# Two attention-and-MLP layers on one core: a new order for the first four tiles, a residual kept in PSUM at the end, and a DMA queue scheduled with new estimates of issue times

## The chip, the cores and the metric

The kernel runs on one core of one Trainium2 chip. The metric is the time of one execution on the device in microseconds (us), lower is better. A profile is of one execution, and its span is a few us shorter than that execution's time. Engine names are those of the profile: PE (TensorE matmul), PEld (its weight load), DVE (VectorE), ACT (ScalarE), POOL (GpSimd), SPq (the queue of DMA issues of the sync engine). "PEclk" is the TensorE clock that was granted, 1.00 being full speed.

## The reference

```python
def reference(A_x, A_wqkv, A_wo, B_x, B_w1, B_b1, B_w2, B_b2):   # x: 1 x 2048 x 512, bf16
    # _A_ref: qkv = x @ wqkv, 32 heads of 16; softmax(q k^T / 4) v; @ wo
    # _B_ref: gelu(layernorm(x) @ w1 + b1) @ w2 + b2, hidden 1376   (it normalises its input once more)
    x = A_x
    x = x + _A_ref(_layernorm(x), A_wqkv, A_wo)                          # "L = 1" in the kernel
    x = x + _B_ref(_layernorm(x), B_w1, B_b1, B_w2, B_b2)
    x = x + _A_ref(_layernorm(x), A_wqkv, A_wo)                          # "L = 3"
    x = x + _B_ref(_layernorm(x), B_w1, B_b1, B_w2, B_b2)
    return x
```

Two times 32 x 2048 x 2048 exponentials make up most of the work.

## The kernel before

The kernel is a generator of instructions. Jobs (Python generators) submit tasks with a priority (the lower number goes first) and with **estimated durations**. A list scheduler plays these estimates forward and, for each engine, takes the ready task of the lowest priority number; if none is ready it takes the one that is ready first. What comes out is a fixed order of some 43,000 instructions, in which each engine waits in program order. The estimates do no work on the chip, but they decide the order.

```python
    def op(self, eng, fn, reads=(), writes=(), same_ok=(), dur=0.3, lat=None):
        ...
        if eng == "sp":                                     # a DMA: dur = time on the queue,
            self.free[eng] = op.t0 + dur
            op.t1 = op.t0 + dur + (2.0 if lat is None else lat)   # lat = from there to the landing
    ...
    def best(self, e):                                      # choice of the next task of engine e
        lim = self.P.free[e] + self.LOOK[e]
        for t in self.pend[e]:
            r = self.task_ready(t)
            if r <= lim: k = (t.prio, t.seq)                # ready: lowest (prio, seq)
            else:        k = (r, t.prio, t.seq)             # none ready: the earliest
    ...
    def dma(self, fn, reads, writes, prio, dur=0.08, lat=None):
        return Task("sp", prio, [I(fn, reads, writes, dur, (), lat)])
```

All DMAs go through one queue. The ones that matter here:

```python
        ld = lambda fn, writes: self.dma(fn, [], writes, 2.0, 0.1, 4.0)            # MLP weights
        ...
        yield self.dma(lambda e: e.dma_start_transpose(xnT, xnr), [RX], [RXT], prio, 0.9)   # tokens
        ...
            # query transposes, one for each segment of (512 queries, 4 heads):
            yield self.dma(... dma_start_transpose(self.qraw..., self.q_scr...), ..., 1.5, 0.9 * sg["W"] / 512)
        ...
    def job_kload(self, hg):        # second attention: keys and values of 12 token tiles come back from DRAM
        yield ("keys", [(k, 3, tt) for k in ("ks", "vs") for tt in range(12)])
        yield self.dma(lambda e: e.dma_start_transpose(self.KT[:, hg:hg + 1, 0:1536], self.k_scr[...]), ..., 1.4, 2.6)
        yield self.dma(lambda e: e.dma_start(self.V[:, hg, 0:12, ...], self.v_scr[...]), ..., 1.4)   # dur 0.08
```

At the start, each of the first four token tiles did keys, queries and values in one job and took the norms of queries and keys in one reduction; the rows of the softmax bound (`qt`, five small operations) went to POOL. In the first attention the other 12 tiles follow behind, while 64 exponentials of the first four tiles' pairs run.

Of the kernel before, what the change touches and what calls it, by code (L numbers as in the profile page):

```python
# [8 lines left out]
BF16 = mybir.dt.bfloat16  # L9
# [442 lines left out]
class Builder:  # L452
# [44 lines left out]
    def alloc(self, es):  # L497
# [44 lines left out]
        self.n2 = t("n2", [128, 2, 64], F32)  # L542
        self.n2k = t("n2k", [128, NT, 32], BF16)
        self.nm = t("nm", [128, 32], BF16)
        self.qy = t("qy", [128, 2, 32], I32)
        self.qt1 = t("qt1", [128, 2, 32], F32)
        self.qt2 = t("qt2", [128, 2, 32], F32)
# [27 lines left out]
        pl["sq"] = Pool(range(3))  # L575
        pl["n2"] = Pool(range(2))
# [17 lines left out]
    def sqs(self, s):  # L594

        if s == 0:
            return self.sq0[:, :].rearrange("p (h c) -> p h c", c=16)
        return (self.h16[:, 8:10, :] if s == 1 else self.OT[:, 6:8, :]).rearrange("p a (h c) -> p (a h) c", c=16)
# [73 lines left out]
    def build_startup_late(self):  # L672
# [4 lines left out]
        def fills():  # L677
# [18 lines left out]
            ld = lambda fn, reads, writes: self.dma(fn, reads, writes, 4.0, 0.4, 5.0)  # L696
# [30 lines left out]
    def flow_weights(self):  # L727
# [3 lines left out]
        ld = lambda fn, writes: self.dma(fn, [], writes, 2.0, 0.1, 4.0)  # L731

        def first(fc):
            M = 128 if fc < nf else self.FLAST
            dst = self.wf[:, fc, 0:4 * M].rearrange("p (c m) -> p c m", m=M)
            return ld(lambda e: e.dma_start(dst, wr1[:, :, fc * 128:fc * 128 + M]), [("wf", fc)])

        def second(L, fc):
            W = self.w2res(L, fc) + ([("wqkv", fc % 3)] if L == 3 else [])
            M = 128 if fc < nf else self.FLAST  # L740
            yield ld(lambda e: e.dma_start(self.w2(L, fc)[0:M, :], self.B_w2[fc * 128:fc * 128 + M, :]), W)
            if fc == nf:
                yield ld(lambda e: e.dma_start(self.w2(L, fc)[M:M + 1, :], self.B_b2.rearrange("(o n) -> o n", o=1)), W)
# [47 lines left out]
    def job_lnqkv(self, L, tiles, prio, later=None):  # L791
# [4 lines left out]
        for i, tt in enumerate(tiles):  # L796
            self.S_.spawn(self.job_qkv_tile(L, tt, slot, i, left, prio + 0.01 * i, "qkv" if later is None else "kv"), prio + 0.01 * i)
# [5 lines left out]
    def job_qkv_tile(self, L, tt, slot, i, left, prio, what):  # L803
        S_ = self.S_
        direct = (L == 1) or tt >= 12
        start = (L == 1 and tt < 4)
        if start:
            xnr, RX = self.dp[:, 4 + tt // 2, (tt % 2) * 512:(tt % 2) * 512 + 512].bitcast(BF16), ("xs", tt)
            xnT, RXT = self.yT[:, :, tt * 128:(tt + 1) * 128], ("yT", tt)
        else:  # L810
            xr = yield ("get", "xn")
            xnr, RX = self.xn[:, xr, :], ("xn", xr)
# [4 lines left out]
        if not start:  # L817
            xs = yield ("get", "xnT")
            xnT, RXT = self.xnT[:, xs, :, :], ("xnT", xs)
        yield self.dma(lambda e: e.dma_start_transpose(xnT, xnr), [RX], [RXT], prio, 0.9)  # L820
        if not start:
            S_.release("xn", xr)
# [7 lines left out]
        def kstore():  # L830
            if direct:
                yield self.dma(lambda e: e.dma_start_transpose(self.KT[:, :, tt * 128:(tt + 1) * 128], self.qks(qs)[:, 1, :]), [QK], [("kt", hg, tt) for hg in range(8)], prio, 1.75)
            else:
                yield self.dma(lambda e: e.dma_start(self.k_scr[tt * 128:(tt + 1) * 128, :], self.qks(qs)[:, 1, :]), [QK], [("kscr", tt)], prio)
            S_.mark(("ks", L, tt))

        def vstore(vs):
            yield self.dma(lambda e: e.dma_start(self.v_scr[tt * 128:(tt + 1) * 128, :], self.vst[:, vs, :]), [("vst", vs)], [("vscr", tt)], prio)
            S_.release("vst", vs)
            S_.mark(("vs", L, tt))  # L840
# [6 lines left out]
        if start:  # L847
            ss = yield ("get", "sq")
        if "k" in what:
# [3 lines left out]
            if start:  # L853
                yield Task("act", prio, [I(lambda e, b=b: e.activation(out=self.sqs(ss)[:, 32:64, :], in_=kdst, func=ACTF.Square), [QK], [("sq", ss, 1)], 0.65)])
            S_.release("mb", b)
            S_.spawn(kstore(), prio)
        if "q" in what:
# [3 lines left out]
            if start:  # L861
                yield Task("act", prio, [I(lambda e: e.activation(out=qdst, in_=qsrc, func=ACTF.Copy, scale=0.25 * YU), [("ps", b)], [QQ], 0.65),
                                         I(lambda e: e.activation(out=self.sqs(ss)[:, 0:32, :], in_=qsrc, func=ACTF.Square, scale=0.25 * YU), [("ps", b)], [("sq", ss, 0)], 0.65)])
            else:
                yield Task("dve", prio, [I(lambda e: e.tensor_scalar(out=qdst, in0=qsrc, scalar1=0.25 * YU, scalar2=None, op0=ALU.mult), [("ps", b)], [QQ], 0.68)])
            S_.release("mb", b)
        if "v" in what:
# [3 lines left out]
            if direct:  # L871
# [3 lines left out]
                if start:  # L875
                    yield Task("act", prio, [I(lambda e: e.activation(out=vdst, in_=psv, func=ACTF.Copy), [("ps", b)], VR, 0.65)])
                else:
                    yield Task("dve", prio, [I(lambda e: e.tensor_copy(out=vdst, in_=psv), [("ps", b)], VR, 0.68)])
# [7 lines left out]
        if not start:  # L886
            S_.release("xnT", xs)
        if not start:
            ss = yield ("get", "sq")
# [7 lines left out]
        if not start:  # L897
            yield Task("dve", prio, [I(lambda e: e.tensor_tensor(out=sq, in0=v4, in1=v4, op=ALU.mult), [("qk", qs, k) for k in range(k0, k1)], SR, 0.12 + 0.0085 * N)])
        yield Task("dve", prio, [I(lambda e: e.tensor_reduce(out=self.n2[:, ns, h0:h1], in_=sq, axis=AX.X, op=ALU.add), SR, [("n2", ns)], 0.12 + 0.017 * N)])
        S_.release("sq", ss)  # L900
        if "k" in what:
            yield Task("dve", prio, [I(lambda e: e.tensor_copy(out=self.n2k[:, tt, :], in_=self.n2[:, ns, 32:64]), [("n2", ns)], [("n2k", tt)], 0.18)])
            S_.mark(("n2k", L, tt))
        if "q" in what:
            yield Task("dve", prio, [I(lambda e: e.tensor_scalar(out=self.qy[:, ns, :], in0=self.n2[:, ns, 0:32].bitcast(I32), scalar1=-0.5, scalar2=RSQRT_MAGIC, op0=ALU.mult, op1=ALU.add), [("n2", ns)], [("qy", ns)], 0.18)])
            y = self.qy[:, ns, :].bitcast(F32)
            a, c, x = self.qt1[:, ns, :], self.qt2[:, ns, :], self.n2[:, ns, 0:32]
            RA, RC, RX = ("qt1", ns), ("qt2", ns), ("n2", ns)
            yield Task("pool", prio, [I(lambda e: e.tensor_tensor(out=a, in0=x, in1=y, op=ALU.mult), [RX, ("qy", ns)], [RA], 0.35)])
            yield Task("pool", prio, [I(lambda e: e.tensor_tensor(out=c, in0=a, in1=y, op=ALU.mult), [RA, ("qy", ns)], [RC], 0.3)])  # L910
            yield Task("pool", prio, [I(lambda e: e.tensor_scalar(out=c, in0=c, scalar1=-0.5, scalar2=1.5, op0=ALU.mult, op1=ALU.add), [RC], [RC], 0.28)])
            yield Task("pool", prio, [I(lambda e: e.tensor_tensor(out=a, in0=a, in1=c, op=ALU.mult), [RA, RC], [RA], 0.3)])
            yield Task("pool", prio, [I(lambda e: e.tensor_scalar(out=pads(self.qks(qs)[:, 0, :])[:, :, 16:17], in0=a.rearrange("p (n o) -> p n o", o=1), scalar1=-MARG, scalar2=0.0, op0=ALU.mult, op1=ALU.add),
                                        [RA], [QQ], 0.4)])
# [3 lines left out]
        if "q" in what:  # L918
            li = L // 2
            if start:  # L920
                yield Task("pe", 0.5, [I(lambda e: e.transpose(self.psbf(self.q0bank)[:, tt * 128:(tt + 1) * 128], self.qks(qs)[:, 0, 0:128], self.ident[:, :]), [QQ, ("ident",)], [("ps", self.q0bank)], 0.1, [("ps", self.q0bank)])])
                S_.mark(("q0", tt))
            yield self.dma(lambda e: e.dma_start(self.q_scr[li, tt * 128:(tt + 1) * 128, :], self.qks(qs)[:, 0, :]), [QQ], [("qscr", L, tt)], prio)
            S_.mark(("qst", L, tt))
        S_.release("qk", qs)

# [22 lines left out]
    def flow_q(self):  # L949
        for sg in self.segs:  # L950
# [6 lines left out]
            else:  # L957
# [3 lines left out]
                               [("qscr", L, tt) for tt in sg["toks"]], [("qraw", s)], 1.5, 0.9 * sg["W"] / 512)  # L961
# [32 lines left out]
    def job_kload(self, hg):  # L994
# [3 lines left out]
                       [("kscr", tt) for tt in range(12)], [("kt", hg, kb) for kb in range(12)], 1.4, 2.6)  # L998
        yield self.dma(lambda e: e.dma_start(self.V[:, hg, 0:12, :, :].rearrange("p k h d -> p k (h d)"), self.v_scr[0:1536, hg * 68:(hg + 1) * 68].rearrange("(k p) c -> p k c", p=128)),
                       [("vscr", tt) for tt in range(12)], [("V", hg, kb) for kb in range(12)], 1.4)  # L1000
# [319 lines left out]
    def job_segend(self, sg):  # L1320
# [20 lines left out]
        if nparts == 2 and part == 0:  # L1341
# [4 lines left out]
            yield Task("pool", 1.2, [I(lambda e: e.tensor_copy(out=M, in_=T[:, :, 0:16]), [RA], [RO] + [("sq", 2, i) for i in (0, 1)], 0.5), I(lambda e: e.tensor_copy(out=den, in_=T[:, :, 16]), [RA], [RD], 0.2)])  # L1346
# [26 lines left out]

    def job_post(self, L, qc):
        S_ = self.S_
        pr = 0.95 if (L, qc) == (1, self.NC - 1) else 2.2
# [28 lines left out]
    def job_yt(self, L, tt, slot, i, left, pr):  # L1405
# [6 lines left out]
        yield self.dma(lambda e: e.dma_start_transpose(self.yT[:, :, i * 128:(i + 1) * 128], self.xn[:, xr, :]), [("xn", xr)], [("yT", i)], pr, 0.9)  # L1412
# [222 lines left out]
```

## Time and profile before

| | before |
|---|---|
| time, median (lowest to highest) | 1698.29 us (1695.0 to 1700.98), 3 runs |
| profiled span | 1695.3 us, mean granted PE clock 0.988 |
| ACT busy / idle in the span | 1580.9 / 114.4 us |
| exponentials of ACT | 1322 in number, idle directly before them 81.6 us |

ACT is the engine to watch. Its busy time in stretches shows where its idle time lies; the columns are the stretch, its length, ACT's busy time with the number of instructions, the PE clock, the DMA share and GB/s:

```profile
0.00:98.00 98.00, 69.35 (x80) 1.00 0.67 137
98.00:130.00 32.00, 20.29 (x19) 0.79 0.48 102
130.00:850.00 720.00, 702.29 (x613) 1.00 0.16 38
850.00:895.00 45.00, 34.43 (x31) 0.92 0.68 114
895.00:1660.00 765.00, 736.58 (x639) 0.99 0.09 22
```

The length less the busy time is the idle time: 28.7, 11.7, 17.7, 10.6 and 28.4 us. The two short stretches lose far more in proportion than the long ones of the bulk. These are the two rows of ACT's timeline that the start and the first short stretch turn on (start, busy time, operation, count; in brackets the idle time before the row and what ended it):

```profile
32.54 10.19 ACT L1113 ACTIVATE PT<-ps 128x1024 bf16<-128x1024 f32 x11 [7.86 <-PE ps L1128]
...
106.21 1.02 ACT L1113 ACTIVATE PT<-ps 128x1024 bf16<-128x1024 f32 x1 [8.05 <-PE ps L1128]
```

The second short stretch is the layer switch, where the queue and the wait of DVE read like this (start, time on the queue, operation, count; then waiter, releaser, total, times, longest):

```profile
843.78 14.85 SPq L997 DMA_TRANSPOSE KT<-k_scr  x7
858.73 9.00 SPq L999 DMA_DIRECT2D V<-v_scr  x7
...
872.02 5.43 SPq L960 DMA_TRANSPOSE qraw<-q_scr  x3
```

```profile
DVE QT L972 <- DMA qraw<-q_scr: 8.6, 1, 8.6
```

All reloads go first, the query transposes last, and DVE stands still for 8.6 us for a query transpose.

### The profile page before, as it was taken

Reading aid. Unit: us, or ns where it says so; the run is one execution under the profiler, and the core shown is the slowest. Engines: PE = TensorE matmul, PEld = TensorE weight load, DVE = VectorE, ACT = ScalarE, POOL = GpSimd, SP = SyncE. Lnnn points to the kernel's source line nnn. Section 1 sums busy time; section 2 is a strip of 40 time slices with the busy share of each in tenths; the row PEclk is TensorE's granted clock in tenths of the full one; section 3 lists DMA queues with packets and bytes.
Section 4 is the critical chain, followed back from the end, with each engine's and each line's share of the span. In section 5 each row is a group of like instructions: output and inputs, shape, how many; then the busy total and the mean of one; then the engine's idle time right before and its main releaser. Section 6 shows DMA issues by size and latency. Waiting matters only on the chain.

```text
span 1695.3 us, 43536 instructions
## 1 busy us (share of the span) xinstructions
PE 1618.0 (95%) x18235; PEld 543.4 (32%) x18235; DVE 1456.1 (86%) x3164; ACT 1580.9 (93%) x1400; POOL 384.0 (23%) x640
## 2 busy tenths in 40 slices
PE   8989999999999999999989999999999999999998
PEld 5222322222222332232223323323222222344444
DVE  6869999988898799988949799988899989988894
ACT  4879999999998999999979999899999999999995
POOL 4045421101211112111122124411011101223220
PEclk9989999999999999999999999999999999999999
DMA  6662000102102211102372230010000100000000
GB/s 165 112 112 64 23 8 8 39 19 56 55 22 48 41 55 33 30 28 44 79 119 55 57 82 20 18 20 8 17 8 8 20 12 8 7 19 7 22 7 14
DMA packets 181249, 66.52 MB, mean 39 GB/s; under 512 B 160859, under 2 KB 175424, under 8 KB 181056
## 3 DMA queue, kind: packets, MB, share of 16 engines
q1 hardware_dynamic: 181056, 63.75, 17.0%
q8 instruction: 146, 2.39, 0.6%
q14 instruction: 47, 0.39, 0.1%
HBM read 19.96 MB, written 15.30 MB: 21 GB/s over the span
## 4 chain that ended last, share of the span: by engine, by line
PE 60%; ACT 30%; DVE 6%; DMA 2%; issue 1%; SPq 1%; POOL 0%; DVEq 0%; POOLq 0%
ACT PT L1113 27%; PE ps L1128 22%; PE ps L1297 17%; PE ps L844 4%; PE ps L1420 4%; PE ps L1458 4%; PE ps L1038 4%; PE ps L1387 3%; DVE dp L1205 2%; DVE dp L1236 2%; ACT h L1450 2%; PE ps L1041 1%; DMA yT<-xn 1%; DVE accT L1327 1%; DMA xnT<-xn 0%
## 5 line engine op out<-in xcount | busy, mean ns | idle before, releaser
L1113 ACT ACTIVATE PT<-ps 128x1024 bf16<-128x1024 f32 (+1 forms) x1322 | 1505.8, 1256 | 81.6 <-PE ps L1128 75.8
L1128 PE MATMUL ps<-QT,KT 32*128 32x512 bf16 (+1 forms) x4608 | 678.4, 359 | 53.1 <-ACT PT L1113 21.3
L1205 DVE TENSOR_SCALAR dp<-ps 128x512 uint16<-128x512 f32 x824 | 557.8, 684 | 121.2 <-PE ps L1128 114.0
L1236 DVE TENSOR_SCALAR dp<-dp 128x1024 uint16<-128x1024 uint16 (+1 forms) x1257 | 490.4, 432 | 10.9 <-PE ps L1297 6.6
L1297 PE MATMUL ps<-PT,V 128*17 128x512 bf16 (+1 forms) x3674 | 472.0, 361 | 0.2 <-DVE accT L1327 0.2
L989 POOL TENSOR_SCALAR vs<-V 128x340 bf16<-128x340 bf16 (+3 forms) x312 | 258.3, 833 | 866.1 <-PE ps L1297 817.4
L1297 PE MATMUL ps<-dp,vs 128*17 128x512 bf16 (+1 forms) x2802 | 408.2, 357 | 0.4 <-DVE dp L1236 0.4
L1128 PEld LDWEIGHTS ps<-QT,KT 32*128 32x128 bf16 x4608 | 178.5, 91 | 578.7 <-issue 172.5
L1297 PE MATMUL ps<-dp,V 128*17 128x512 bf16 (+1 forms) x934 | 195.7, 358 | 2.4 <-DVE accT L1327 2.2
L1038 PE MATMUL ps<-wqkv,zw 128*32 128x256 bf16 x4432 | 188.2, 275 | 0.8 <-DVE accT L1327 0.8
L1297 PEld LDWEIGHTS ps<-PT,V 128*17 128x17 bf16 x3674 | 111.3, 88 | 114.9 <-issue 102.2
L1297 PEld LDWEIGHTS ps<-dp,vs 128*17 128x17 bf16 x2802 | 102.4, 89 | 111.2 <-issue 95.3
L1038 PEld LDWEIGHTS ps<-wqkv,zw 128*32 128x32 bf16 x4432 | 105.8, 96 | 80.3 <-issue 60.8
L1420 PE MATMUL ps<-yT,wf 128*128 128x512 bf16 (+3 forms) x396 | 104.8, 369 | 4.8 <-DMA yT<-xn 3.9
L844 PE MATMUL ps<-wqkv,xnT 128*128 128x512 bf16 x336 | 95.2, 391 | 8.8 <-DMA xnT<-xn 8.8
L1327 DVE STREAM_TRANSPOSE accT<-ps 128x512 f32<-128x512 f32 (+1 forms) x88 | 58.1, 661 | 23.5 <-PE ps L1297 22.2
L1444 DVE TENSOR_SCALAR h<-ps,b1c 128x512 bf16<-128x512 f32 (+2 forms) x88 | 61.7, 701 | 9.3 <-PE ps L1420 8.8
L1387 PE MATMUL ps<-wo,OT 128*128 128x512 bf16 x240 | 68.0, 387 | 0.2 <-DVE dp L1205 0.2
L1297 PEld LDWEIGHTS ps<-dp,V 128*17 128x17 bf16 x934 | 48.1, 88 | 43.4 <-issue 26.7
L1420 PEld LDWEIGHTS ps<-yT,wf 128*128 128x128 bf16 (+1 forms) x396 | 28.5, 100 | 59.2 <-issue 30.1
L972 DVE TENSOR_SCALAR QT<-qraw,scl,qbias 128x512 bf16<-128x512 bf16 (+1 forms) x87 | 37.3, 431 | 10.3 <-DMA qraw<-q_scr 10.0
L1367 DVE STREAM_TRANSPOSE OT<-ob 128x512 bf16<-128x512 bf16 (+1 forms) x72 | 45.9, 639 | 0.1
(154 smaller groups left out, 801.9 us busy)
## 6 DMA issues: line engine op xcount, KB each, us to landing
wf<-in_B_w_dram SPq DMA_DIRECT2D x90, 128.0 KB, 2.5
q_scr<-qk SPq DMA_DIRECT2D x22, 256.0 KB, 2.2
k_scr<-qk SPq DMA_DIRECT2D x12, 256.0 KB, 2.0
out_dram<-xres SPq DMA_DIRECT2D x16, 128.0 KB, 1.7
v_scr<-vst SPq DMA_DIRECT2D x12, 136.0 KB, 2.0
V<-v_scr SPq DMA_DIRECT2D x8, 204.0 KB, 4.9
wqkv<-in_A_wqkv_dram SPq DMA_DIRECT2D x3, 512.0 KB, 4.2
q_scr<-h SPq DMA_DIRECT2D x6, 256.0 KB, 3.1
```

The costliest lines, as they stand in the source:

```text
L844: yield Task("pe", prio, [I(lambda e, c=c: e.matmul(self.ps[:, b, :], lhsT=xnT[:, c, :], rhs=self.wqkv[:, c, which * 512:which * 512 + 512 ...
L989: yield Task("pool", 0.8, [I(lambda e, k=k: e.tensor_scalar(out=self.vs[:, q, k - 1, i:i + n, :], in0=src, scalar1=WSHIFT[k], scalar2=None ...
L1038: P.op("pe", lambda e, p=p: e.matmul(self.ps[p:p + 32, b, 0:w], lhsT=self.zw[:, 0:32], rhs=rhs[:, 0:w], start=st, stop=st, skip_group_chec ...
L1113: S_.submit(Task("act", 1e-5 * gi, [I(lambda e, pt=pt, n=n, b0=b0: e.activation(out=self.PT[:, pt:pt + n, :], in_=self.ps[:, b0:b0 + n, :] ...
L1128: return [I(lambda e, kb=kb, i=i: e.matmul(self.ps[:, b, i * W:(i + 1) * W], lhsT=self.KT[32 * hp:32 * hp + 32, hg, kb * 128:(kb + 1) * 12 ...
L1205: self.S_.submit(Task("dve", 0.0, [I(lambda e: e.tensor_scalar(out=self.dp[:, u, w * 512:(w + 1) * 512], in0=self.ps[:, b, :], scalar1=BIT ...
L1236: yield Task("dve", pr, [I(lambda e, k=k, v=v: e.tensor_scalar(out=self.dp[:, v, 0:N], in0=self.dp[:, u, 0:N], scalar1=float(SHIFT[k]), sc ...
L1297: ops.append((i, I(lambda e, hp=hp, v=v, ap=ap[:, i * W:(i + 1) * W], first=first and i == 0, W=W: e.matmul(self.ps[32 * hp:32 * hp + 17, ...
L1327: yield Task("dve", 0.3, [I(lambda e: e.transpose(self.accT[:, a, 0:W], self.ps[:, ACCB, 0:W]), [("ps", ACCB)], [RA], 0.15 + 0.53 * W / 512)])
L1387: yield Task("pe", pr, [I(lambda e, hg=hg, i=i, b=b: e.matmul(self.ps[:, b, :], lhsT=self.OT[:, hg, i * 128:(i + 1) * 128], rhs=self.wo[:, ...
L1420: yield Task("pe", pr, [I(lambda e, c=c: e.matmul(self.ps[0:M, b, off:off + W], lhsT=self.w1(fc, c), rhs=self.yT[:, c, 0:W], start=(c == 0 ...
L1458: yield Task("pe", pr, [I(lambda e, fc=fc, i=i, b=b: e.matmul(self.ps[:, b, :], lhsT=self.gt(fc, i, W), rhs=self.w2(L, fc), start=(fc == 0 ...
```

## The change

The intent has three parts. **Start:** in the first four tiles, keys and their norms come first, queries next, values last; the last tile's bound rows go to DVE, and there are more buffers for squares and norms. **Queue:** the DMAs get new estimates, meant to be the issue times of a trace. Also, MLP weights fall behind (priority 3.0), query transposes pass the reloads (1.3 against 1.4); the MLP of the third unit of the first layer is raised from 2.2 to 1.6. **Tail:** the last tokens' residual is put into PSUM by an identity matmul, so that two adds fall away, and 14 output projections no longer go ahead of the last attention matmuls. Cut to its core:

```diff
-        ld = lambda fn, writes: self.dma(fn, [], writes, 2.0, 0.1, 4.0)
+        ld = lambda fn, writes, dur, prio: self.dma(fn, [], writes, prio, dur, 3.5)
-            return ld(lambda e: e.dma_start(dst, wr1[...]), [("wf", fc)])
+            return ld(lambda e: e.dma_start(dst, wr1[...]), [("wf", fc)], 0.75, 3.0)
-        yield self.dma(lambda e: e.dma_start_transpose(xnT, xnr), [RX], [RXT], prio, 0.9)
+        yield self.dma(lambda e: e.dma_start_transpose(xnT, xnr), [RX], [RXT], prio, 1.25)
-            (key transposes 1.75, key, value and query stores 0.08)
+            (key transposes 2.4,  key, value and query stores 0.45)
-                               [...qscr...], [("qraw", s)], 1.5, 0.9 * sg["W"] / 512)
+                               [...qscr...], [("qraw", s)], 1.3, 0.1 + 1.1 * sg["W"] / 512)
-                       [...kscr...], [...kt...], 1.4, 2.6)
+                       [...kscr...], [...kt...], 1.4, 2.0)
-                       [...vscr...], [...V...], 1.4)
+                       [...vscr...], [...V...], 1.4, 1.3, 3.5)
+    def post_prio(self, L, qc):
+        return 0.95 if (L, qc) == (1, self.NC - 1) else 1.6 if (L, qc) == (1, self.NC - 2) else 2.2
 ... first four tiles
+    def job_first_tile(self, tt, slot, i, left, prio):
+        ...                       # three jobs for each tile
+        S_.spawn(keys(), prio)            # its tasks at prio - 0.3: 4 matmuls, copy, square, reduce of 32 norms
+        S_.spawn(queries(), prio)         # 4 matmuls, copy and square on ACT, reduce; bound rows on "dve" if tt in (3,)
+        S_.spawn(values(), prio + 1.0)    # 4 matmuls, copy on ACT
 ... tail
+        yield Task("pe", 1.5, [... matmul(ps[b], lhsT=ident, rhs=xres[tt], start=True, stop=False ...)])
-            yield Task("pe", pr, [... matmul(ps[b], OT, wo, start=(hg == 0), stop=(hg == 7)) ...])
+            yield Task("pe", pr if h0 == 7 else 1.5, [... matmul(ps[b], OT, wo, start=False, stop=(hg == 7)) ...])
-        yield Task("dve", pr, [... tensor_tensor(xres = ps + xres) ...])
-        yield Task("dve", pr, [... bn_stats(st, in_=xres) ...])
+        yield Task("dve", pr, [... bn_stats(st, in_=ps) ...])
 ... (second MLP matmuls add into the same bank; the two last adds become copies, one on DVE, one on ACT)
```

## The prediction

> **What bounds the kernel now.** I read the page first (busy shares, 40 slices), then ScalarE's (ACT) groups with shapes kept apart, then the ACT exponentials by stretches of 10 and 20 us to find where they stop, then the timelines of ACT and of the DMA queue (SPq) around each stop, and the chain for the two ends of the kernel.
>
> ```profile
> PE 1618.0 (95%) x18235; PEld 543.4 (32%) x18235; DVE 1456.1 (86%) x3164; ACT 1580.9 (93%) x1400; POOL 384.0 (23%) x640
> L1113 ACT ACTIVATE PT<-ps 128x1536 bf16<-128x1536 f32 x629 | 930.6, 1479 | 46.1 <-PE ps L1128 40.7
> L1113 ACT ACTIVATE PT<-ps 128x1024 bf16<-128x1024 f32 x692 | 723.5, 1053 | 35.5 <-PE ps L1128 35.1 <-PE ps L942 0.2
> ```
>
> The bulk is softmax exponentials on ACT. The union of all of them is 1506 us of 1695. PE's 95% contains filler matmuls (188 us at one line alone), so the real limit in the bulk is ACT, with DVE and PE close behind. ACT idles 1695.3 - 1580.9 = 114 us in all, 81.6 us of it directly before exponentials. The change cannot shorten an exponential, so what it can win lies in that idle time and in the work before the first and after the last exponential.
>
> ```profile
> 100.00:120.00 20.00, 10.39 (x10) 0.66 0.42 89
> ...
> 510.00:520.00 10.00, 6.78 (x7) 0.83 0.28 44
> ...
> 870.00:880.00 10.00, 2.82 (x3) 0.73 0.66 130
> ...
> 1070.00:1080.00 10.00, 6.72 (x7) 1.00 0.12 27
> 1130.00:1140.00 10.00, 7.17 (x8) 0.70 0.23 47
> ...
> 1520.00:1530.00 10.00, 5.63 (x5) 0.66 0.10 21
> ```
>
> These are stretches (first line exponentials alone, the others all of ACT): length, busy time and count, granted PE clock, DMA share, GB/s. Outside them ACT is mostly above 9 in 10. Almost every hole has a lowered PE clock, so PE had stopped too. The queue shows why for the first big one:
>
> ```profile
> 89.35 0.56 SPq L697 DMA_DIRECT2D bst<-in_B_b_dram  x1
> 89.96 0.23 SPq L698 DMA_DIRECT2D bst<-in_B_b_dram  x1
> 90.23 1.75 SPq L701 DMA_DIRECT2D wo<-in_A_wo_dram  x4
> 92.02 8.13 SPq L736 DMA_DIRECT2D wf<-in_B_w_dram  x11
> 100.26 3.85 SPq L820 DMA_TRANSPOSE xnT<-xn  x3
> ```
>
> For 10.9 us the single queue issues weights that nobody needs for hundreds of us, while transposes of normalised tokens stand behind them. PE, in order, waits 6.9 us for the first transpose, and ACT waits 8.05 us before its exponential at 106.2, then 2.0 us more while PE is at a low clock.
>
> **What the Trainium skill says.** "DMA: Bandwidth & Descriptors", Anatomy of one DMA: a semaphore wait of a DMA happens on the issuing sequencer, before dispatch, and the fixed cost is about 2 us, mostly completion. The trace agrees on head-of-line blocking (above), but gives the issue cost itself as the problem: 8.13/11 = 0.74 us per weight load, 6.01/4 = 1.5 us per token transpose, 9.00/7 = 1.29 us per V reload. The scheduler in the kernel assumed 0.1, 0.9 and 0.08. "TensorE: Matmul & The Clock Gate", HAM oscillation: an idle gap of over about 3.4 us halves the PE clock. The trace agrees: four matmuls that take 0.97 us in the chain took 1.89 us after the 6.9 us gap. "VectorE: DVE Perf Modes", Why PSUM operands drop a tier: a PSUM source caps the mode. The trace agrees: the normalise from SBUF takes 0.41 us for 128x512, a PSUM read about 0.68. "PSUM — Partial Sum Buffer", The four PSUM rules: seed a bank through PE with an identity matmul. No run before the change shows it; the change does exactly that.
>
> **The change, part by part.**
>
> *1. Start.* Now the first exponential is at 32.54 us. Chain: transposes land from 13.1, 48 projection matmuls of 0.219 us run to 23.6, ACT squares and copies to 24.7, a 1.2 us reduce to 25.4, the key-norm chain to 28.1, and the last query tile's GpSimd rows to 28.3. Then DVE, in order, waits 2.1 us for token loads in bn_stats placed ahead of QT, which comes only at 31.4. After: keys and queries are 32 of the 48 matmuls, so the last query is ready near 13.2 + 32*0.219 = 20.2 instead of 23. Norms are split into two 0.67 us reduces, and the last tile's five row operations move from POOL (0.33 us steps, 25.8 to 28.3) to DVE at perhaps 0.17 each. DVE is then the limit of the start: 4 tiles x (0.69 copy + 2*0.67 reduce + 0.35 small) = 9.5 us from 14.2 gives 23.7, plus 1.1 for the scale chain and about 0.8 for the rows, so 25.6. QT (0.5) and scores (0.4) with semaphore steps give a first exponential near 27, 5.5 us earlier. The stage after it, to 98 us, runs PE at 9 to 10 tenths and DVE at 8 to 9, so it must move as a whole. I count **5 us**.
>
> *2. The queue at 90 to 106.* Weight loads get 0.75 us and priority 3.0, so transposes (1.25 us, more urgent) go first. The hole is 20 - 10.39 = 9.6 us at 100 to 120 plus 1.8 at 98 to 100, 11.4 us. All three compute engines stand still in it, so nothing is merely hidden. I count **10 us**.
>
> *3. Second-layer reload at 850 to 890.* Eight K reloads and eight V reloads occupy the queue from 843.8 to 871.1 and hold a query transpose. ACT loses 5.55 and 2.36 us around 877 and 1.7 us at 855, about 10 in all. Now V reloads are modelled at 1.3 us, query transposes have priority 1.3 before the reloads' 1.4, and the third unit's post-processing is raised from 2.2 to 1.6. The queue work of 27 us stays; only its order moves. I count **6 us**.
>
> *4. Transposes before the MLP* (holes at 510, 1130, 1520: 3.2, 2.8 and 3.0 + 1.7 us). They are now modelled at 1.25 us instead of 0.9, but the last one still needs 4.4 us from issue to landing, which the model underestimates. I count **4 us** of some 11.
>
> *5. Tail.* Fourteen output-projection matmuls (3.13 us) now precede the last 16 attention matmuls:
>
> ```profile
> 1670.54 3.13 PE ps L1523 x14
> 1673.67 0.57 PE ps L1297 x15
> ...
> 1676.25 1.29 DVE xres L1525 x2
> 1677.54 1.19 DVE st L1529 x2
> ...
> 1691.85 0.69 DVE xres L1503
> ```
>
> With priority 1.5 they give way. Exponentials end at 1671.66, so attention could end near 1672.3 instead of 1674.2: about 1.5 us, some lost because the fourteen plus two identity matmuls then fill PE beside the 2.1 us DVE chain. The residual in PSUM removes two adds (1.29 us) from the chain, and bn_stats and normalise from PSUM give back about 0.1 + 0.3. The last two copies on two engines instead of two adds on one save 0.6. Sum 1.5 + 0.9 + 0.6 = **3 us**.
>
> Sum: 5 + 10 + 6 + 4 + 3 = 28 us. Every changed duration reorders all later instructions, and real timing will not follow the model in new places either. For this I take back 1 us, and get 1698 - 27 = **1671 us**.
>
> **Rivals.** *(a) The bulk takes it back.* DVE and PE are at about 9 tenths from 120 to 300 us, so an earlier start would meet them. For it: DVE at 18.3 to 19.8 of 20 us there. Against: in the two big holes all of them idle together, so that removed time is real. It would keep the start's gain from the end: 1676 to 1680. *(b) A new misplaced wait.* The order of 43,000 instructions changes, and one wrong DMA estimate costs 5 to 11 us, as the trace shows twice. One new such hole makes 1678 to 1682. For it: reload and token-load latencies are still under the measured ones (2 us assumed for a 7.1 us load of tokens). Against: the largest errors are mended. *(c) All holes close.* The yT holes and the one at 1070 go too, and both big ones entirely: 5 + 11 + 10 + 10 + 3 + 3 = 42 us, 1656. *(d) Only priorities matter little and the reload stays bound by its 27 us of queue:* part 3 gives 1 us, 1676.
>
> **Range and chances.** Between (b) with a weak start (1687) and nearly (c) (1659) I expect 8 in 10 cases. Faster by over 2% needs below 1664.3, 34 us, which needs the reload and the yT holes both mostly closed: 0.22. Slower by over 2% would need 60 us of new holes: 0.01. Within 2%: 0.77.
>
> **What would show it.** First exponential near 27 us (step 1; above 30 it failed). No ACT gap over 3 us between 85 and 115, and weight issues after the token transposes (step 2). ACT busy at 860 to 890 above 27 of 30 (step 3). Gaps at the yT transposes under 2 us (step 4). Last exponential to end of span 20.5 us or less instead of 23.6 (step 5). If these hold and the span is still above 1685, rival (a) took it: exponentials between 120 and 840 us would have more idle time before them than now. A single new hole of 5 us or more with a DMA as releaser would be rival (b).

## More of the kernel before

Scores (`ps<-QT,KT`) are exponentiated mostly by ACT (`PT<-ps`), in part by DVE with a bit trick (`dp<-ps`, then three shifted copies), whose values are multiplied with scaled copies `vs<-V` made by POOL:

```python
        yield Task("pool", 0.8, [I(lambda e, k=k: e.tensor_scalar(out=self.vs[...], in0=src, scalar1=WSHIFT[k], ...),
                                   ..., 0.15 + 0.06 * n, ...) for k in (1, 2, 3)])   # n blocks of 68 columns
```

## The result, and the profile after

| | before (same runs) | after |
|---|---|---|
| time, median (lowest to highest), 4 runs each | 1698.94 us (1695.0 to 1700.98) | **1681.22 us** (1679.88 to 1683.74) |
| profiled span, mean PE clock | 1695.3 us, 0.988 | 1678.1 us, 0.993 |
| ACT busy / idle | 1580.9 / 114.4 us | 1587.0 / 91.1 us |
| first exponential | 32.54 us | 27.50 us |
| last exponential to the end | 23.6 us | 21.2 us |

The ratio is 0.990, with a 95% interval of 0.9878 to 0.9922: 17.7 us less by the medians, within 2%. A ratio here is the mean time of one kernel's fast runs over that of the other's of the same rounds, so it isn't quite the ratio of the medians that are quoted beside it.

First the page: the busy shares and, from the groups with shapes kept apart, ACT's two kinds of exponentials with the idle time before them.

```profile
PE 1613.1 (96%) x18524; PEld 544.3 (32%) x18524; DVE 1441.4 (86%) x3145; ACT 1587.0 (95%) x1405; POOL 379.6 (23%) x635
```

```profile
L1179 ACT ACTIVATE PT<-ps 128x1536 bf16<-128x1536 f32 x631 | 936.4, 1484 | 38.5 <-PE ps L1194 32.0
L1179 ACT ACTIVATE PT<-ps 128x1024 bf16<-128x1024 f32 x694 | 728.3, 1057 | 24.0 <-PE ps L1194 23.4
```

Idle before exponentials fell from 81.6 to 62.5 us. ACT's busy time rose by 6.1 us, though: DVE took 814 score halves in place of 824, and ACT the ten others (the time in which at least one exponential of ACT runs grew from 1505.8 to 1511.3 us). So 23.3 us of idle time went, and 6.1 us of it was paid back in work; 23.3 - 6.1 = 17.2 us is the difference of the spans. By stretch, as above:

```profile
0.00:98.00 98.00, 70.38 (x81) 1.00 0.63 129
98.00:130.00 32.00, 23.66 (x21) 0.89 0.68 127
130.00:850.00 720.00, 702.50 (x611) 0.99 0.17 40
850.00:895.00 45.00, 44.23 (x40) 1.00 0.65 97
895.00:1660.00 765.00, 740.70 (x643) 1.00 0.09 21
```

The layer switch (850 to 895) went from 10.6 us idle to 0.8, by far the largest item. Around 98 to 130 us only 3.4 us came free, though the first exponential is 5 us earlier. Here is ACT's timeline at the start; the brackets give the idle time before a row and its releaser:

```profile
27.50 7.44 ACT L1179 ACTIVATE PT<-ps 128x1024 bf16<-128x1024 f32 x8 [4.23 <-PE ps L1194]
...
98.81 4.63 ACT L1179 ACTIVATE PT<-ps 128x1536 bf16<-128x1536 f32 x4 [4.89 <-PE ps L1194]
...
126.17 1.45 ACT L1179 ACTIVATE PT<-ps 128x1536 bf16<-128x1536 f32 x1 [5.77 <-PE ps L1194]
```

The old hole of 8.05 us before the exponential at 106.2 is now 4.89 us, at 98.8. A new one of 5.77 us stands at 126.2. The queue did do what the change meant, weights behind transposes:

```profile
93.02 5.13 SPq L817 DMA_TRANSPOSE xnT<-xn  x3
...
105.88 2.22 SPq L736 DMA_DIRECT2D wf<-in_B_w_dram  x4
```

But a wait of the queue itself took their place. These are, in order, the queue's longest wait in 84 to 130 us, DVE's wait behind it, and POOL's timeline before it:

```profile
SPq L893 <- POOL qt L905: 6.5, 1, 6.5
```

```profile
122.25 0.41 DVE L785 TENSOR_SCALAR xn<-xres,mv,rs 128x512 bf16<-128x512 bf16 x1 [5.11 <-DMA xnT<-xn]
```

```profile
96.10 10.75 POOL L1055 TENSOR_SCALAR vs<-V 128x68 bf16<-128x68 bf16 x24
...
107.30 5.68 POOL L1055 TENSOR_SCALAR vs<-V 128x68 bf16<-128x68 bf16 x12
```

A query store (L893) waits in the queue for bound rows that POOL makes late, because 36 copies `vs<-V` go first at 0.42 us apiece (the scheduler's estimate is 0.15 + 0.06 = 0.21). Token transposes wait behind the store, DVE for a free buffer behind those, PE (4.6 us) behind DVE, and ACT behind PE. A segment is the work for 512 queries and 4 heads; I count the segments from 0 by the transposes of their results. Segment 8 ends at 128.6 us against 134.0 before, but segment 11 only 0.4 us earlier than before and segment 13 later by 1.6: by 190 us the early gain is gone.

At the layer switch the queue now reads:

```profile
839.64 7.40 SPq L1063 DMA_TRANSPOSE KT<-k_scr  x4
...
849.50 2.91 SPq L1026 DMA_TRANSPOSE qraw<-q_scr  x2
...
861.35 5.35 SPq L1065 DMA_DIRECT2D V<-v_scr  x5
```

Query transposes pass between the reloads, and no wait of DVE for one is left. The windows that the prediction showed for the later holes:

```profile
510.00:520.00 10.00, 9.79 (x10) 1.00 0.13 36
...
1130.00:1140.00 10.00, 10.00 (x10) 1.00 0.22 41
1520.00:1530.00 10.00, 9.85 (x10) 1.00 0.04 8
```

### The profile page after: what moved, and what is told of

The parts are those of the page before. It is cut to its first block, busy times and chain, and to the rows that moved or that the text cites. A ratio compares the mean times of both kernels' runs of the same rounds, so it can differ in the third digit from the quotient of the medians.

```text
span 1678.1 us, 44066 instructions
## 1 busy us (share of the span) xinstructions
PE 1613.1 (96%) x18524; PEld 544.3 (32%) x18524; DVE 1441.4 (86%) x3145; ACT 1587.0 (95%) x1405; POOL 379.6 (23%) x635
## 4 chain that ended last, share of the span: by engine, by line
PE 56%; ACT 31%; DVE 7%; POOL 2%; DMA 2%; issue 1%; SPq 0%; POOLq 0%; DVEq 0%
ACT PT L1179 28%; PE ps L1194 21%; PE ps L1363 16%; PE ps L1490 5%; PE ps L1104 4%; PE ps L1528 4%; PE ps L840 4%; PE ps L1457 3%; DVE dp L1271 3%; DVE dp L1302 2%; ACT h L1520 1%; DMA xnT<-xn 1%; POOL vs L1055 1%; DMA qraw<-q_scr 1%; ACT L1179 0%
## 5 line engine op out<-in xcount | busy, mean ns | idle before, releaser
L1179 ACT ACTIVATE PT<-ps 128x1024 bf16<-128x1024 f32 (+1 forms) x1326 | 1511.3, 1260 | 62.5 <-PE ps L1194 55.4
L1271 DVE TENSOR_SCALAR dp<-ps 128x512 uint16<-128x512 f32 x814 | 550.7, 683 | 119.9 <-PE ps L1194 111.8
L1302 DVE TENSOR_SCALAR dp<-dp 128x1024 uint16<-128x1024 uint16 (+1 forms) x1242 | 483.0, 430 | 14.3 <-PE ps L1363 9.7
L1363 PE MATMUL ps<-dp,vs 128*17 128x512 bf16 (+1 forms) x2766 | 403.6, 357 | 2.3 <-DVE dp L1302 2.1
L1104 PE MATMUL ps<-wqkv,zw 128*32 128x256 bf16 x4712 | 202.8, 278 | 0.9 <-DVE accT L1393 0.9
L1104 PEld LDWEIGHTS ps<-wqkv,zw 128*32 128x32 bf16 x4712 | 115.2, 97 | 82.3 <-issue 64.3
L1490 PE MATMUL ps<-yT,wf 128*128 128x512 bf16 (+3 forms) x396 | 100.8, 360 | 0.2
L905 POOL TENSOR_TENSOR qt<-n,qy 128x32 f32<-128x32 f32 x31 | 9.5, 307 | 156.2 <-DVE qy L901 156.0
```

The lines of the kernel that those rows point to most:

```text
L1104: P.op("pe", lambda e, p=p: e.matmul(self.ps[p:p + 32, b, 0:w], lhsT=self.zw[:, 0:32], rhs=rhs[:, 0:w], start=st, stop=st, skip_group_chec ...
L1179: S_.submit(Task("act", 1e-5 * gi, [I(lambda e, pt=pt, n=n, b0=b0: e.activation(out=self.PT[:, pt:pt + n, :], in_=self.ps[:, b0:b0 + n, :] ...
L1271: self.S_.submit(Task("dve", 0.0, [I(lambda e: e.tensor_scalar(out=self.dp[:, u, w * 512:(w + 1) * 512], in0=self.ps[:, b, :], scalar1=BIT ...
L1302: yield Task("dve", pr, [I(lambda e, k=k, v=v: e.tensor_scalar(out=self.dp[:, v, 0:N], in0=self.dp[:, u, 0:N], scalar1=float(SHIFT[k]), sc ...
L1363: ops.append((i, I(lambda e, hp=hp, v=v, ap=ap[:, i * W:(i + 1) * W], first=first and i == 0, W=W: e.matmul(self.ps[32 * hp:32 * hp + 17, ...
L1490: yield Task("pe", pr, [I(lambda e, c=c: e.matmul(self.ps[0:M, b, off:off + W], lhsT=self.w1(fc, c), rhs=self.yT[:, c, 0:W], start=(c == 0 ...
```

## The experiments

Twelve kernels ran, each timed in five rounds against the kernel before. All were correct. The kernel before had medians of 1697.7, 1695.92 and 1696.18 us (11, 11 and 12 runs; the last shares many runs with the second).

**e1, the start alone.** The kernel before with the new first four tiles; all queue durations and priorities old, tail old.

```diff
+            if L == 1 and tt < 4:
+                self.S_.spawn(self.job_first_tile(tt, slot, i, left, prio), prio)
+                continue
```

> The kernel before with only the new first tiles (keys, then queries, values last; bigger pools); DMA estimates, priorities and tail as before. Theory A (the start is absorbed): the first exponential comes at 27 to 28 us, but the last key norm of the sixteen still at 91 to 94 us and the weight loads still block the queue behind it, so the time falls by at most 2 us. Theory B (the parts add up as predicted): the time falls by about 5 us and the first exponential of the second part (1536 wide) comes 4 to 6 us earlier than 106.2.

Measured: 1699.05 us, ratio 1.0008 (0.9974 to 1.0042). The first exponential came at 27.8 us, but ACT then had a gap of 6.6 us at 44.6 (PE waited 5.0 us for a token transpose that stood behind two query transposes in the queue) and one of 10.8 us before 112.0. Theory A was right in the time (under 2 us) but not in its path: the last key norm came at 97.8 us and not at 91 to 94, and the second scale at 102.3 us (before: 96.6). An earlier start alone brought nothing that these runs resolve: the 64 pair exponentials were done sooner, and the 12 later tiles came even later.

**e2, the queue alone.** The kernel before with all new durations and with the priorities of weights and query transposes; the third unit's priority, the start and the tail are old.

```diff
-   ... [("wf", fc)])              # MLP weights: priority 2.0, estimate 0.1
+   ... [("wf", fc)], 0.75, 3.0)
-   ... [("qraw", s)], 1.5, 0.9 * sg["W"] / 512)
+   ... [("qraw", s)], 1.3, 0.1 + 1.1 * sg["W"] / 512)
```

> The kernel before with only the DMA durations and DMA priorities of the change. Theory A: the holes at 98 to 106 and at 870 to 884 us shrink, a new one with DMA as releaser may stand near 120; gain 8 to 14 us. Theory B: 20 us (10 + 6 + 4 of the prediction).

Measured: 1696.32 us, ratio 0.9992 (0.9955 to 1.0028). Both theories missed. The hole at 98 to 106 fell from 8.0 to 3.7 us and the gaps at 840 to 900 from 9.6 to 4.7 us, as wished; but the store behind POOL opened 4.9 us at 120.9, and the rest was lost in other places. The last key norm came at 98.2 us and the second scale at 102.1. (The profiled run is the slowest of the six, 1705.41 us, so its gaps are those of a poor run.)

**e3, the tail alone.** The kernel before with the new tail.

```diff
-        yield Task("dve", pr, [... tensor_tensor(xres = ps + xres) ...])
+        yield Task("pe", 1.5, [... matmul(ps[b], lhsT=ident, rhs=xres[tt], start=True, stop=False) ...])
```

> The kernel before with only the new last tokens (residual put into PSUM through PE, lower priority of the early output projection, last copies on two engines). Both theories: last exponential to end of span falls from 23.6 to about 21 us, the time by 2 to 3 us; everything up to 1600 us is unchanged within 1 us, as the scheduler places instructions in order of time.

Measured: 1697.45 us, ratio 0.9993 (0.9959 to 1.0027). In the profile the last exponential is 22.0 us before the end instead of 23.6, where about 21 was expected; the 2 to 3 us of time that were expected are not resolved.

**e4, weights later.** The kernel after, whose second group of weight loads (the MLP's) waits until all 16 query stores are issued. The order on PE, DVE, ACT and POOL comes out the same as in the kernel after; only the queue differs.

```diff
-        yield ("keys", [("kv", 1, tt) for tt in range(self.NT)] + [("wld",)])
+        yield ("keys", [("kv", 1, tt) for tt in range(self.NT)] + [("wld",)] + [("qst", 1, tt) for tt in range(self.NT)])
```

> The changed kernel, but the first MLP weight loads wait until all sixteen query stores have been issued, so that no weight load lies between the transposes at 105 to 125 us. Theory A (weight traffic delays the transpose that DVE waits 5.1 us for at 117 to 122): that wait falls below 2 us and the time by 4 to 6 us. Theory C (the bulk between 100 and 225 us is bound by DVE, PE and GpSimd work and takes back whatever is won before): the wait goes, but the attention segment that ends at 206 us ends within 1.5 us of that, and the time changes by less than 1.5 us.

Measured: 1679.88 us (1678.99 to 1680.57), ratio to before 0.9894. The gap before 126.7 stayed, 6.1 us, and DVE's wait behind it too, 5.4 us, without one weight load near it. Both theories had expected that wait to go, so neither was right. So weight traffic isn't its cause, and the queue's wait for POOL, now 10.2 us, came into view.

**e5, a longer estimate for POOL's copies.** The kernel after with one estimate changed. It is right for copies of one block (0.40 us, measured 0.42) and still short for five: 0.80, where 128x340 took 1.09; the 0.83 of the expectation is a mean over mixed shapes.

```diff
-   ... 0.15 + 0.06 * n, ...
+   ... 0.30 + 0.10 * n, ...
```

> The changed kernel with one estimate of the scheduler put right: GpSimd's scaled copies of V, assumed at 0.15 + 0.06n us (n key tiles), get 0.30 + 0.10n, as the trace has them (0.41 us at n = 1, 0.83 at n = 5). No operation is added or removed. Theory D (after the queue was mended, GpSimd, believed twice as fast as it is, makes query rows late; the query store then blocks the DMA queue for 6.5 us, and transposes, DVE, PE and ACT behind it): the 5.8 us gap before the exponential at 126 us goes below 2.5 us, the waits of DVE for GpSimd at 150 to 180 us (3.6 us) shrink, and the time falls by 4 to 9 us, to 1672 to 1677. Theory C (the bulk between 100 and 225 us is bound by total work): the gap only moves and the time stays within 1.5 us of the changed kernel's 1681.

Measured: **1674.5 us** (1667.8 to 1679.84), ratio 0.9873 (0.9847 to 0.9898), the fastest of all. In ACT's timeline, a gap of 4.7 us before 101.9 (the one that was 4.89) is the last for long: the row over the place of the hole at 126 is 17 exponentials without a break, and no gap of 0.9 us or more follows until 797:

```profile
110.82 19.62 ACT L1179 ACTIVATE PT<-ps 128x1024 bf16<-128x1024 f32 x17 [0.42 <-PE ps L1194]
```

What Theory D named came: the gap is gone, DVE's wait for POOL at 150 to 190 us fell from 3.6 to 1.0 us, and the time lies in its 1672 to 1677. Segment 11 ends 10.7 us earlier than in the kernel after, segment 27 16.9 us. But the profiled run is one of the slow ones of the six (1679.46 us), and by its end it is level with the kernel after (spans of 1677.6 and 1678.1): most of the lead was given back later, gaps of 5.4 us in sum at 840 to 900 among it, which the kernel after doesn't have. The 6.7 us between the medians lie within the scatter that e8 shows.

**e6, the third unit's priority back at 2.2.** The kernel after otherwise.

```diff
-        return 0.95 if (L, qc) == (1, self.NC - 1) else 1.6 if (L, qc) == (1, self.NC - 2) else 2.2
+        return 0.95 if (L, qc) == (1, self.NC - 1) else 2.2
```

> The changed kernel with the third unit's post-processing back at priority 2.2 (as before). If this priority is what empties the stretch at 850 to 890 us, the hole of 5 us or more at 870 to 885 comes back and the time rises by 5 to 8 us. If the V reload's duration and the query transposes' priority did it, the time stays within 2 us.

Measured: 1689.08 us (1686.32 to 1695.33), ratio to before 0.9968. Gaps at 840 to 900: 2.3 and 2.4 us, the same two as in e2. The time rose by 7.9 us, about as the first reading said, but no hole of 5 us or more came back, so neither reading is confirmed; and 7.9 us lies within the scatter of e8.

**e7, start and queue together.** The kernel after without the third unit's priority and with the old tail.

```diff
 (as e6, and the tail of the kernel before)
```

> The changed start and the changed DMA estimates, without the third unit's priority and without the changed tail. Alone, neither of the two gained anything (1699.1 and 1696.3 against 1697.7). Theory E (they need each other: with the old queue the early start runs into a 6.6 us wait for a token transpose at 38 to 44 us and a 10.8 us gap before 112; with the old start the new queue meets late key norms): together 8 to 12 us, so 1686 to 1690. Theory F (the gain is that of the third unit's priority and of chance in the order): together within 3 us of 1697.

Measured: 1690.77 us (1688.58 to 1695.62), ratio 0.9972 (0.9951 to 0.9993). Two parts that gave nothing each gave 4 to 5 us together, less than Theory E said and more than Theory F; by the next experiment, this too is within the scatter. Against e6 the tail would be worth 1.7 us, about what e3's profile shows.

**e8, a placebo.** The kernel after with one estimate moved by 0.01 us, the layer norm's normalise step.

```diff
-   ... [("x", tt), ("mv", c), ("rs", slot)], [dres], 0.39)])
+   ... [("x", tt), ("mv", c), ("rs", slot)], [dres], 0.40)])
```

> A control: the changed kernel with one estimate of the scheduler moved by 0.01 us (the normalisation of a token tile, 0.39 to 0.40 us; the trace has 0.41). It has no meaning for the hardware and only reshuffles the order. It shows how much of a difference between two schedules is chance: I expect within 3 us of the changed kernel's 1681; if it is 6 us or more away, differences of that size between other variants say nothing about their cause.

Measured: **1705.24 us** (1699.67 to 1710.08), ratio to before 1.005, that is 24 us above the kernel after. The expectation missed by a factor of eight. Up to 850 us the ends of the segments stand within 8 us of the kernel after; then, in ACT's timeline:

```profile
860.22 10.71 ACT L1179 ACTIVATE PT<-ps 128x1536 bf16<-128x1536 f32 x9 [8.02 <-PE ps L1194]
876.32 6.88 ACT L1179 ACTIVATE PT<-ps 128x1024 bf16<-128x1024 f32 x6 [5.40 <-PE ps L1194]
```

The next attention can't begin before the last key norms, and DVE's timeline has these (second kernel: after) at

```profile
856.02 0.18 DVE L884 CAST n2k<-n 128x32 bf16<-128x32 f32 x1
```

```profile
842.61 0.17 DVE L884 CAST n2k<-n 128x32 bf16<-128x32 f32 x1
```

13.4 us apart. At the last value store 672 exponentials were done in e8 and 665 in the kernel after. I read this as seven exponentials that were left to cover the switch; e9 to e11 did not bear that out.

This placebo changed the question: how much of 17.7 us is the change, and how much a draw, that is, one of many orders of which an irrelevant edit picks one?

**e9 and e10, two placebos of the kernel before** (0.40 and 0.38 in place of 0.39).

```diff
-   ... [dres], 0.39)])
+   ... [dres], 0.40)])      # e9;  0.38 in e10
```

> The kernel before, with one figure of the scheduler changed by 0.01 (its estimate of one VectorE layer-norm instruction, 0.39 to 0.40), the same edit that cost the kernel after 24 us. Theory S (the order of the instructions is a lottery worth up to 20 us either way, drawn mostly at the layer switch at 840 to 890 us): this kernel differs from the kernel before by 5 to 20 us, up or down, and the sum of the ScalarE gaps at 840 to 895 us goes with how many exponentials are done when the last value rows are stored: 0 to 10 us at 665 or 666 done (before: 9.7 at 666), 4 to 6 us at 668 to 670, 12 us or more at 672. Rival R (the kernel before is robust and only the changed one is brittle): within 4 us of before, so 1692 to 1700, with the same gaps 1.7, 5.6 and 2.4 at 856 to 881.

> The kernel before with the same figure at 0.38 in place of 0.39. Theory S: differs by 5 to 20 us from before, up or down, and not by the same amount as the twin at 0.40. If the gain of the change (17 us) is nothing but a lucky draw, one of the two twins should come to 1685 or less; if the change is worth something of its own, both stay above 1688. Rival R: within 4 us of before.

Measured: 1711.28 us (1703.91 to 1714.89), ratio 1.0078 (1.0052 to 1.0105), and 1711.98 us (1702.88 to 1714.82), ratio 1.0094 (1.0072 to 1.0117). So Theory S holds (15.1 and 15.8 us away, inside its 5 to 20) and Rival R fails: the kernel before is as brittle as the one after. Of both kernels, the draw that was published is the best of its three. Both twins stay above 1688, which the expectation named as a sign that the change is worth something of its own. My count of exponentials done at the last value store, which was to say how large the gaps are, failed: both have 670 done, for which I expected 4 to 6 us, and both lose 20 to 21 us at 840 to 900. In e9 the queue repeats the kernel before (seven key reloads, then values, query transposes from 880.6 on), DVE waits 5.8 us for one of them, and a second thing is added: the output projection of the last unit stands in front of the scores in PE's order, with a DVE add between its matmuls. These two rows are from e9's chain of work at 863 us (start, duration, what); one such pair stands before them and one follows:

```profile
863.80 1.92 PE ps L1387 x8
...
865.74 0.70 DVE xres L1389
```

ACT waits 12.2 us through it. In e10 it waits 12.4 us at the same place, through the same matmuls and adds.

**e11, a second placebo of the kernel after** (0.38).

> The kernel after with the same figure at 0.38. Theory S: anywhere from 1675 to 1705, with the gaps at 840 to 895 us by the count of exponentials done at the last value store, as said for the twin of the kernel before: none or under 2 us at 665 or 666, 4 to 6 us at 668 to 670, 12 or more at 672. Rival (the twin at 0.40 was a single bad case and the gain is firm): 1677 to 1685.

Measured: 1683.03 us (1679.15 to 1686.72), ratio 0.9923 (0.9902 to 0.9943). At 840 to 900 it lost 7.9 us with 672 done, where I expected 12 or more: the count failed again. The time lies in the range of Theory S and in that of its rival, so it decides nothing between them. The first exponential was at 31.2 us in this draw, and no cost of that is seen in the total.

**e12, the placebo of e5** (0.40 and the longer POOL estimates).

> The kernel after with the true GpSimd durations in the scheduler (1674.5 us, the best so far) and the figure at 0.40. The cause shown for the hole at 126 us (GpSimd copies take twice their estimate, so the query store waits in the queue) says that no ScalarE gap over 1.5 us comes back between 102 and 200 us whatever the draw; a gap there of over 3 us would refute it. Its total is a draw as with the others: 1670 to 1695, and under 1681 if the repair carries through.

Measured: 1693.99 us (1686.48 to 1694.41), ratio 0.9975 (0.9952 to 0.9997). No gap of over 1.5 us between 102 and 200 us, as expected of the shown cause. The total is over the 1681 that I named: in the profiled run the end alone takes 33.7 us after the last exponential, against 23.0 in e5, while PE still has MLP matmuls of the unit before to do. The store behind POOL still waits 3.4 us in the queue, but nothing that is needed soon stands behind it. The two draws with the longer POOL estimates have a mean of 1684.2 us, against 1689.8 for the three of the kernel after: e5 is the version to keep, as the fastest measured, not as a proven better rule.

### What the twelve say together

Because the total is a draw, I read the named gaps over all fourteen kernels, sorted by the queue's estimates. The third column is the first wide gap of ACT after 98 us; the fourth is the largest gap of over 2 us from 115 to 200 us; the fifth is the sum of gaps of 0.9 us or more at 840 to 900.

| kernel | queue | gap at 98 to 112 | gap at 115 to 200 | gaps at 840 to 900 | query transposes | time (median) |
|---|---|---|---|---|---|---|
| before | old | 8.0 | none | 9.6 | after the reloads | 1696 to 1699 |
| e1 | old | 10.8 | none | 10.6 | after | 1699.05 |
| e3 | old | 8.4 | none | 9.8 | after | 1697.45 |
| e9 | old | 8.8 | none | 21.1 | after | 1711.28 |
| e10 | old | 7.9 | none | 20.0 | after | 1711.98 |
| after | new | 4.9 | 5.8 | 0 | between | 1681.22 |
| e4 | new | 4.5 | 6.1 | 0 | between | 1679.88 |
| e2 | new | 3.7 | 4.9 | 4.7 | between | 1696.32 |
| e6 | new | 4.8 | 3.6 | 4.7 | between | 1689.08 |
| e7 | new | 4.7 | 5.7 | 4.7 | between | 1690.77 |
| e8 | new | 4.6 | 7.1 | 13.4 | between | 1705.24 |
| e11 | new | 3.4 | 2.3 | 7.9 | between | 1683.03 |
| e5 | new, POOL longer | 4.7 | none | 5.4 | between | 1674.5 |
| e12 | new, POOL longer | 4.6 | none | 6.0 | between | 1693.99 |

Three things hold in every draw. With the old queue the first gap is 7.9 to 10.8 us, with the new one 3.4 to 4.9. The gap at 115 to 200 is there in all seven kernels with the new queue and the old POOL estimate, and in none of the others. And DVE's wait of 5.5 to 8.8 us for a query transpose at the switch is there in all five with the old queue; of the nine with the new one only e11 has one, of 2.0 us. The size of the gaps at the switch overlaps (0 to 13.4 against 9.6 to 21.1), so the difference of the means there, 14.2 less 5.2 = 9.0 us, has a wide scatter about it, and after and e4 are one draw. Nor is all of it the queue's: in e9 and e10 12 us of the gaps are the output projection in front of the scores, and the other three old kernels have a mean of 10.0.

The traces also say what is left of the first gap. In all nine kernels with the new queue it ends 1.8 to 2.2 us after the second scale (after: scale at 96.6, exponential at 98.81), in the five with the old queue 9.5 to 12.8 us after it (before: 96.6 and 106.21). So the old queue held ACT long after the scale was there, and with the new one the gap ends right behind the scale.

For the whole change, three draws of the kernel before have a mean of about 1706.5 us (1696.2, 1711.3, 1712.0) and three of the kernel after 1689.8 (1681.2, 1705.2, 1683.0). The difference, 16.7 us, is as large as the measured 17.7; but with standard deviations of 9 and 13 us in three draws each, its standard error is about 9 us. For these two kernels as they are the gain is sure; that the change as such, over all orders, is worth 17 us is plausible and not shown.

One rival was not tested: the granted PE clock. It differs between runs of one and the same kernel, and the time goes with it: in 23 runs the kernel before took from 1689.82 us at 0.992 to 1710.33 at 0.977, an estimate of 12 us for each 0.01. The kernel after had 0.991 to 0.993 in the runs that were scored. At 0.991 to 0.992 the kernel before took 1689.8 and 1690.2 us and the kernel after 1680.5 to 1683.7: 6 to 10 us apart in place of 17.7. The lower clock may itself come of the waits (in the kernel before it was 0.50 from 99.8 to 113.4 us, right after PE's gap of 6.9 us), and then it belongs to the gain; no run separates the two. It doesn't explain the scatter away: at 0.992 e8 took 1700.24 us.

## Why the prediction was right or wrong

The total was 1681 against 1671 predicted, inside the range; "within 2%" was right. In part that is luck: of the three draws of the kernel after, e8 (1705) lies outside the range of 1659 to 1687. Of the signs that the prediction named, two came (the first exponential at 27.5 us; ACT busy for 29.2 of 30 us at 860 to 890), and so did the gaps of under 2 us at the yT transposes in the windows shown. Two did not: a gap of ACT of 4.89 us stayed between 85 and 115, where none over 3 was to be, and the last exponential is 21.2 us before the end, not 20.5 or less. By its steps:

**1. Start (5 us): right in its own number, wrong in the sum.** The first exponential moved from 32.54 to 27.50, as worked out. "The stage after it ... must move as a whole" is what failed. The last key norm of the first 16 tiles came at 92.5 us instead of 92.1 and the second scale at 96.6 in both kernels, so nothing of the 5 us had reached them. In the other kernels this norm came between 92.0 and 98.2 us; what sets it isn't shown. In e1 the term alone gave nothing that could be resolved. This is rival (a), met at 98 us rather than in the bulk.

**2. Queue at 90 to 106 (10 us): right mechanism, size off.** The gap fell by 3.2 us (8.05 to 4.89); with the smaller gaps right behind it the hole was 11.5 us and is 4.9, so some 6 us came free against 10. What stays of it ends right behind the second scale. Then rival (b), which the prediction described, took back 5.8 us at 126: a wait of the queue put there by an engine whose estimate the change had left at half the true time. e4 excluded the weights, and e5 and e12 confirmed POOL. The reading of the clock here needs a limit: half clock followed PE's gap of 6.9 us, but in the same trace also a gap of 1.9 us (at 513.6, half clock from 516.2 to 519.6), and at 1134.0 to 1140.8 us it came with no gap of PE over 1.5 us. So that PE had stopped in almost every hole with a lowered clock isn't shown. And 0.74 and 1.5 us for a weight load and a token transpose are means of rows with gaps and some long ones in them; the medians are 0.51 and about 1.25.

**3. Layer switch (6 us): right and larger.** ACT's idle time there fell from 10.6 to 0.8 us. What the new queue did in every draw is to let the query transposes pass the reloads, which took away DVE's wait for them; e2 has about 5 us of this (9.6 to 4.7) without the third unit's priority, and e6 and e7 have the same 4.7. What brought the rest, from 4.7 to 0, isn't shown: with the third unit's priority the gaps at 840 to 900 were 0, 0, 5.4, 6.0, 7.9 and 13.4 us. Rival (d) was wrong for the kernel after; e8, with the same parts, lost 13.4 us there, so the size is luck in part.

**4. Token transposes before the MLP (4 us): the gaps at 510, 1130 and 1520 closed**, worth 3.0 + 2.8 + 4.2 = 10 us of busy time in these windows against 4 predicted, but in e1 and e10 all three are gone too, with the old estimate of 0.9, and e11 has four gaps of 1.5 to 1.9 us at 1517 to 1535 with the new one. I can't put them down to the 1.25.

**5. Tail (3 us): 2.4 in the profile** (23.6 to 21.2), 1.6 in e3, 1.7 us of time between e6 and e7. With the new tail it was 21.2 to 23.0 us in seven of eight kernels, with the old one 23.3 to 25.8 in all six, so the new tail is shorter; the eighth, e12, took 33.7, with MLP matmuls of the unit before still to do.

What the prediction didn't have at all is the term of the order itself. It took back 1 us "for this" and gave the range a width of 28 us for other reasons; an edit without any effect on the work moved the time by 1.8 to 24 us. And the sum counted idle time only: ten score halves moved from DVE to ACT cost 5.5 us of the 23.3 us that were freed.

## What to carry to other kernels

When a scheduler turns estimates into a fixed order, first move one estimate by an irrelevant amount and measure: here that showed a scatter of up to 24 us, under which a single comparison of 5 us means nothing. Judge such a change by waits with a named releaser that come and go in every draw, not by the total. Note the granted clock of every run beside its time. And where durations of one resource are corrected toward traced values, correct those of its neighbours too, since the next lie in the model (POOL at half its time) puts the next wait at the head of the same queue.

## What the Trainium skill lacked or had wrong

- "GPSIMD Engine Reference", section "3.1 Elementwise — side-by-side cycle accounting", gives about 1.8 cycles for each element at 1.2 GHz as the best case and a measured total for one large add, but no fixed cost of a small instruction. In the kernel after a tensor_scalar of bf16 took 423 ns for 128x68, 671 for 128x136, 786 for 128x204 and 1088 for 128x340, which from the first to the last is an estimate of 2.4 ns a column and 0.26 us fixed, both above an estimate by the page (68 x 1.8 / 1.2 = 102 ns for the smallest, without dispatch).
- "DMA: Bandwidth & Descriptors", section "DMA Transpose (X-bar)", lists constraints of the DMA transpose but not how long it holds the queue (other sections of the page have a bandwidth, and sequencer cycles in a comparison with a later chip). Here one token transpose of 128x512 held it for about 1.25 us, and the key reloads of 1536 tokens for 1.3 to 3.6 us each (14.85 us for seven). With a single queue for all DMAs, such times decide what stands behind what.
- No page speaks of how far a fixed order itself scatters the time: up to 24 us of 1681 for a change of 0.01 us in one estimate.
